# Attention and an MLP in one kernel: w_out products two units at a time, bank by bank, and a new order at the start and around the splitting of x

## The chip, the cores and the metric

The kernel runs on one core of one Trainium2 chip. The metric is device time in microseconds (us); times of a kernel are the median of several runs. Engines are named as in the profile: PE (TensorE matmul), PEld (its weight loads), DVE (VectorE), ACT (ScalarE), POOL (GpSimd), SP (SyncE, which issues all DMAs here).

## The reference

Causal attention with a decay, over 8 batches of 8 heads, 576 positions, 64 features per head, and then a two-layer MLP with a gate on 4608 tokens. Cut to what matters:

```python
scores = np.matmul(q, k.T) / 8                     # per batch and head, 576 x 576
cum = np.cumsum(np.log(np.clip(f, 1e-4, 1.0)), -1)
scores = scores + cum[:, None] - cum[None, :]      # causal: -1e9 above the diagonal
attn = exp(scores - max) / (sum + 1e-9)
x = (attn @ v) as (4608 tokens, 512)
h = x @ w_in                                       # 512 -> 2048
g = h * erf(softplus(h))
out = g @ w_out                                    # 2048 -> 512
```

## The kernel before, in words

The program has one instruction stream per engine. For PE, DVE, ACT and POOL the order of the stream is the order in which the Python code makes the instructions; each engine works through its stream in order and waits on semaphores. Only SP's stream, the DMAs, is ordered by the framework's scheduler, and it too is worked through in order: a DMA that waits for a buffer holds up all that stand behind it.

**Start.** `fd[0]` and `fd[1]` are the rows of `f` for the first two heads, broadcast to 128 partitions; `fr` is all of `f` on 64 partitions. From each, `log_clipped` (clip on DVE, log on ACT, L324 and L325) and `decay` (a running sum and a scaling on DVE, L329 and L330) make the decays. Those of the first pair of heads stay in SBUF (`c0`). Those of all heads (`cum`) are written to DRAM (`cum_d`, L482) and read back for each further pair of heads, broadcast (`c`, L344). `idle_products` (L476) are transposes of a constant that nobody reads: they keep PE running while it would have nothing to do.

**Attention** runs over 64 half pairs of heads, t = 0 to 63, as a pipeline: in iteration t stand `scores(t)` (PE, L362 and L367), `reduce(t)` (DVE, L383: adds the decays, takes the extreme), `exps(t-1)` (ACT, L395), `normalize(t-2)` (POOL, L405), `transposes(t-3)` (PE, L417) with `evacuate(t-3)` (ACT L426, DVE L422 and L424), `values(t-4)` (PE, L444) and `store(t-5)`. An even iteration transposes four banks through a ring of three, so its last bank waits for ACT's copy of its first. From t = 4 on each iteration also does a quarter of a `convert`: a piece of w_in or w_out, loaded as 64-bit floats (`wraw`, L279), is made into two float32r parts, high and low: step 0 on ACT (L289), 1 to 3 on DVE (L293, L298, L300, L303, L306) and POOL (L307).

**The MLP** (class `Moe`) works on units: 128 of the 2048 features for one block of 512 tokens. There are 14 visits of token blocks, ten with 8 units and four with 16: 144 units. For a unit j:

- `up(j)` on PE: 12 matmuls of 128x512 (L133) into one PSUM bank `ph` (ring of 4); x and the weights are split in a high and a low part, and three of the four products are made.
- `softplus(j)` and `erf(j)` on ACT (L138, L141). The two need different function tables, so several units share one change of tables (`self.ends`).
- `gate(j)`: DVE multiplies e by h (L147, after which the bank `ph` is free), makes the high part `gh` (L149), POOL the low part `gl` (L150); `gh` and `gl` have rings of 4.
- `down(j)` on PE: 12 matmuls (L169 to L171), three into each of the four banks y0 to y3, which gather a whole visit. `finish` copies the four banks out at the end of a visit (L197, L199) and stores them (L202); visits over half of the features are stored as `part_d` and added in later.

`step()` makes step j: `up(j)`, then the downs due, erf of the units due, softplus(j), the gates due, `finish`, and `split_x`. The tables `ends`, `gates` and `downs` say at which step. Before, units go in groups of three (two at either end): their erfs come at the step after the group's last up, their gates one step each from there on, and each down two steps after its gate. x of the next visit is asked for four units ahead (`want_x`), loaded in two halves through one buffer `xr` (L113), and split by ACT (`xh`, L120) and POOL (`xl`, L121). During the first 32 steps after the attention, two convert steps for the second half of the weights follow each step. `wraw` and the outputs `yo` share a ring of two buffers (`wide4`).

Of the kernel before, what the change touches and what calls it, by code (L numbers as in the profile page):

```python
# [11 lines left out]
F32 = mybir.dt.float32  # L12
# [10 lines left out]
B, H, S, D = 8, 8, 576, 64  # L23
# [44 lines left out]
class Moe:  # L68
# [8 lines left out]
    def __init__(self, tc, xt_d, out, xp, wide4):  # L77
        self.tc, self.nc = tc, tc.nc
        self.xt_d, self.out, self.xp, self.wide4 = xt_d, out, xp, wide4
        first, second, every = (list(range(*r)) for r in ((2 * NU1,), (2 * NU1, NF), (NF,)))  # L80
        self.visits = ([(c, first) for c in range(HALF)] + [(c, second) for c in range(HALF)]
                       + [(c, every) for c in range(HALF, NCH)])
        self.units = [(v, a) for v, (c, feats) in enumerate(self.visits) for a in feats]
        n = len(self.units)
        self.ends, self.gates, self.downs = {}, defaultdict(list), defaultdict(list)
        at = 0
        for size in [2] + [3] * ((n - 6) // 3) + [2, 2]:
            self.ends[at + size] = range(at, at + size)
            for k in range(size):
                self.gates[at + size + k].append(at + k)  # L90
                self.downs[at + size + k + 2].append(at + k)
            at += size
        assert at == n
        self.steps = max(self.downs) + 1
        self.w, self.x, self.e, self.gp, self.y = {}, {}, {}, {}, {}
        self.ps, self.raw, self.part, self.queue = {}, [], {}, []
        self.at = 0
# [52 lines left out]
        nc.gpsimd.tensor_tensor(out=gl, in0=e_, in1=gh.bitcast(F32), op=ALU.subtract)  # L150
        self.gp[j] = gh, gl

    def down(self, j):
        nc = self.nc
        v, a = self.units[j]
        c, feats = self.visits[v]
        gh, gl = self.gp.pop(j)
        wh, wl = (self.w[a // 2][:, i, a % 2 * DM:a % 2 * DM + DM] for i in (2, 3))
        if a == feats[0]:
            self.y[v] = [self.ps_y.tile([P, DM], F32, name=f"y{v}_{tb}", tag=f"y{tb}") for tb in range(4)]  # L160
            if a:
                self.part[v] = [self.wide4(f"part{v}_{b}").rearrange("p (a e) -> p a e", a=2) for b in range(2)]
                for b in range(2):
                    nc.sync.dma_start(out=self.part[v][b], in_=self.part_d[2 * c + b])
        y = self.y[v]
        first, last = a == feats[0], a == feats[-1]
        for tb in range(4):
            cs = slice(tb * P, tb * P + P)
            nc.tensor.matmul(out=y[tb], lhsT=gh[:, cs], rhs=wh, start=first, stop=False)  # L169
            nc.tensor.matmul(out=y[tb], lhsT=gh[:, cs], rhs=wl, start=False, stop=False)  # L170
            nc.tensor.matmul(out=y[tb], lhsT=gl[:, cs], rhs=wh, start=False, stop=last)  # L171
            if j == len(self.units) - 1:
                self.finish_last(y[tb], c * TB + tb * P)

    def finish_last(self, y, row):
# [31 lines left out]
    def step(self):  # L207
        j, n = self.at, len(self.units)
        self.at += 1
        if j < n:  # L210
            self.up(j)
            self.want_x(self.units[min(j + 4, n - 1)][0])
            self.load_x()
        for i in self.downs[j]:
            self.down(i)
        if j in self.ends:
            for i in self.ends[j]:
                self.erf(i)
            self.nc.scalar.preload_act_table_set(SOFTPLUS)
        if j < n:  # L220
            self.softplus(j)
        for i in self.gates[j]:
            self.gate(i)
        for i in self.downs[j]:
            self.finish(i)
        self.split_x()


@with_exitstack
def attention_moe(ctx, tc, q2, k2, vp, f, w_in, w_out, out):  # L230
# [84 lines left out]
    with ExitStack() as ph:  # L315
# [147 lines left out]

        fd = [wk.tile([P, S], F32, name=f"fd{j}", tag=f"pt{j}", bufs=1) for j in range(2)]
        nc.sync.dma_start(out=fd[0], in_=f[0, 0].partition_broadcast(P))
        load(0)
        nc.sync.dma_start(out=fd[1], in_=f[0, 1].partition_broadcast(P))
        fr = wk.tile([B * H, S], F32, name="fr", tag="xo")
        nc.sync.dma_start(out=fr, in_=f.rearrange("b h s -> (b h) s"))
        todo = pieces[1]  # L470

        def idle_products(t, n):
# [2 lines left out]
            for i in range(n):  # L475
                nc.tensor.transpose(out=b[:, i % 4 * P:(i % 4 + 1) * P], in_=ident, identity=ident)  # L476

        def all_decays():
            log_clipped(fr)
            cum = wk.tile([B * H, S], F32, name="cum", tag="xo")  # L480
            decay(cum, fr)
            nc.sync.dma_start(out=cum_d, in_=cum)  # L482
            load(1)
            load(2)
            load_weight(0)

        idle_products("", 16)
        log_clipped(fd[0])
        decay(pairs[0][2][:, 0], fd[0])
        log_clipped(fd[1])  # L490
        for t in range(NH + 5):
            there = [0 <= t - n < NH for n in range(6)]
            p, half = divmod(t, 2)
            if half == 0 and 0 < t < NH - 4:
                load(p + 2)
            if half == 0 and there[2]:
                load_values(p - 1)
            if NH <= t < NH + 4:
                moe.step()
            if there[2]:  # L500
                normalize(t - 2)
            if there[5]:
                store(t - 5)
            if there[0]:
                scores(t)
                if t < 3:
                    idle_products(t, 18)
            if there[1]:
                exps(t - 1, 0)
            if there[0]:  # L510
                reduce(t, 0)
                if t == 0:
                    decay(pairs[0][2][:, 1], fd[1])
            if there[3]:
                for a in range(3):
                    transposes(t - 3, a)
                evacuate(t - 3, 0)
            if there[3] and len(BANKS[(t - 3) % 2]) == 4:
                transposes(t - 3, 3)
            if there[4]:  # L520
                values(t - 4)
            if there[1]:
                exps(t - 1, 1)
            if there[0]:
                reduce(t, 1)
                if t == 0:
                    all_decays()
            if there[3]:
                for a in range(1, len(BANKS[(t - 3) % 2])):
                    evacuate(t - 3, a)  # L530
            if t >= 4 and todo:
                convert(*todo.pop(0))
            if NH - 4 <= t < NH - 2:
                moe.want_x(0)
                moe.load_x()
                moe.split_x()
            if t == NH - 1:
                early.close()
                moe.ep = moe_pools.enter_context(tc.tile_pool(name="ep", bufs=2, side="right"))
                moe.ps_h = moe_pools.enter_context(tc.tile_pool(name="ps_h", bufs=4, space=PSUM, side="right"))  # L540
# [46 lines left out]
```

## Time and profile before

| | us |
|---|---|
| median of 3 runs (lowest, highest) | 1155.87 (1155.82, 1157.66) |
| profiled execution, its own time | 1156.91 |
| its span, first to last instruction | 1155.1 |
| PE busy | 1134.1 |

PE is busy in 98% of the span and its weight loads in 80%; no other engine is in more than 54%. By stages, from the windows of the trace:

| stage | us | PE busy | ACT busy | DVE busy | granted clock |
|---|---|---|---|---|---|
| 0 to 30 (start) | 30 | 24.12 | 12.02 | 16.30 | 1.00 |
| 60 to 300 (attention) | 240 | 240.00 | 191.72 | 202.37 | 1.00 |
| 318 to 325 | 7 | 4.51 | 6.24 | 4.59 | 0.76 |
| 530 to 1130 (MLP, weights ready) | 600 | 600.00 | 240.59 | 170.46 | 1.00 |
| 1130 to 1156 (end) | 26 | 19.84 | 5.81 | 4.27 | 0.96 |

A busy PE still may run slower or faster per matmul, since matmuls overlap: what one costs is read from the distance of their starts, not from the length of one.

### The profile page before, as it was taken

The page shows a single profiled execution, that of the slowest core. Times are in us where ns is not written, and L with a number is a line of the kernel's source. Part 1 is how long each engine was busy: PE and PEld are TensorE (multiplying, and loading weights), DVE is VectorE, ACT ScalarE, POOL GpSimd, SP SyncE. Part 2 cuts the span into 40 slices and gives each one's busy share as a digit, 9 for nine tenths or more (in the row PEclk, how much of TensorE's full clock was granted, in tenths as well). Part 3 has the DMA queues.
Part 4 walks back from the last instruction along what each step waited for, and adds up shares of the span by engine and source line. Part 5 has one row for each costly group of instructions (what it writes and reads, how often), then busy time and mean ns, then how long its engine had stood idle before and what let it go on. Part 6 is the DMA issues. An engine that isn't in the chain of part 4 may idle for free.

```text
span 1155.1 us, 19541 instructions
## 1 busy us (share of the span) xinstructions
PE 1134.1 (98%) x7334; PEld 927.9 (80%) x7334; DVE 565.2 (49%) x1475; ACT 624.4 (54%) x1251; POOL 461.1 (40%) x532
## 2 busy tenths in 40 slices
PE   8999999999989999999999999999999999999998
PEld 6888888888877878778888888888888888888886
DVE  5788888888846576565233132222321322322221
ACT  3878878787786565664444344433342443243342
POOL 2556565555654445344342342332232232232121
PEclk9999999999999999999999999999999999999999
DMA  7677777777622133131031130230010010000001
GB/s 261 206 241 258 243 231 253 237 243 234 198 98 92 54 111 108 57 113 70 19 110 40 71 110 19 91 110 1 37 37 1 37 37 1 37 19 1 37 1 37
DMA packets 57726, 120.05 MB, mean 104 GB/s; under 512 B 4768, under 2 KB 20128, under 8 KB 57632
## 3 DMA queue, kind: packets, MB, share of 16 engines
q1 hardware_dynamic: 57632, 118.80, 31.4%
q8 instruction: 58, 0.95, 0.3%
q14 instruction: 36, 0.29, 0.1%
HBM read 94.52 MB, written 24.26 MB: 103 GB/s over the span
## 4 chain that ended last, share of the span: by engine, by line
PE 90%; DVE 3%; DMA 3%; ACT 2%; POOL 1%; issue 1%; SPq 0%; POOLq 0%; DVEq 0%; ACTq 0%
PE ph L133 32%; PE y L169 11%; PE y L171 11%; PE y L170 11%; PE s L362 8%; PE o L444 8%; PE t L417 7%; PE s L367 2%; DMA wraw<-in_w_in_dram 1%; POOL xl L121 1%; DVE pr L383 1%; DMA k<-in_k_dram 0%; DVE e L147 0%; ACT L289 0%; ACT L141 0%
## 5 line engine op out<-in xcount | busy, mean ns | idle before, releaser
L133 PE MATMUL ph<-xh,w 128*128 128x512 f32 x1152 | 381.7, 392 | 5.7 <-DVE e L147 5.7
L150 POOL TENSOR_TENSOR gl<-e,gh 128x512 fp32r<-128x512 f32 x144 | 186.8, 1298 | 418.9 <-DVE gh L149 414.4
L138 ACT ACTIVATE e<-ph 128x512 f32<-128x512 f32 x144 | 86.1, 598 | 385.1 <-PE ph L133 380.3
L133 PEld LDWEIGHTS ph<-xh,w 128*128 128x128 f32 x1152 | 217.2, 189 | 56.6 <-DVE e L147 5.9
L147 DVE TENSOR_TENSOR e<-e,ph 128x512 f32<-128x512 f32 x144 | 98.1, 681 | 327.0 <-ACT e L141 326.8
L169 PE MATMUL y<-w,gh 128*128 128x512 f32 x576 | 228.9, 397 | 0.0
L171 PE MATMUL y<-w,gl 128*128 128x512 f32 x576 | 228.0, 396 | 0.0
L170 PE MATMUL y<-w,gh 128*128 128x512 f32 x576 | 227.6, 395 | 0.0
L133 PE MATMUL ph<-xl,w 128*128 128x512 f32 x576 | 225.4, 391 | 0.0
L405 POOL TENSOR_SCALAR pr<-pr,st 128x576 f32<-128x576 f32 (+4 forms) x320 | 164.7, 535 | 117.8 <-DVE st L401 102.0
L395 ACT ACTIVATE pr<-pr,st 128x576 f32<-128x576 f32 (+3 forms) x320 | 176.5, 556 | 3.6 <-DVE st L383 3.5
L383 DVE CUSTOM_DVE_ANT_0 pr<-s,c 128x576 f32<-128x576 f32 (+3 forms) x320 | 136.8, 487 | 52.6 <-PE s L367 39.2
L171 PEld LDWEIGHTS y<-w,gl 128*128 128x128 f32 x576 | 108.7, 189 | 27.0
L170 PEld LDWEIGHTS y<-w,gh 128*128 128x128 f32 x576 | 108.2, 188 | 26.1
L169 PEld LDWEIGHTS y<-w,gh 128*128 128x128 f32 x576 | 108.0, 188 | 24.4
L133 PEld LDWEIGHTS ph<-xl,w 128*128 128x128 f32 x576 | 108.4, 188 | 22.7
L149 DVE CAST gh<-e 128x512 fp32r<-128x512 f32 x144 | 92.2, 640 | 66.3 <-PE y L170 52.4
L362 PE MATMUL s<-k,q 64*128 64x320 f32 (+4 forms) x768 | 110.3, 411 | 4.5 <-DVE st L383 2.5
L417 PE MATMUL t<-ident,pr 128*128 128x128 f32 x800 | 103.9, 275 | 4.2 <-ACT pt L426 2.5
L426 ACT COPY pt<-t 128x512 f32<-128x512 f32 x128 | 73.7, 577 | 61.1 <-PE t L417 61.1
L444 PE MATMUL o<-pt,v 128*64 128x128 f32 (+1 forms) x1920 | 103.8, 261 | 0.0
L444 PEld LDWEIGHTS o<-pt,v 128*64 128x64 f32 x1920 | 94.9, 138 | 9.5 <-DVE st L383 4.9
(53 smaller groups left out, 992.2 us busy)
## 6 DMA issues: line engine op xcount, KB each, us to landing
v<-in_vp_dram SPq DMA_DIRECT2D x32, 576.0 KB, 6.2
c<-cum_d SPq DMA_DIRECT2D x62, 288.0 KB, 5.0
xr<-xt_d SPq DMA_DIRECT2D x28, 512.0 KB, 3.4
q<-in_q_dram SPq DMA_DIRECT2D x32, 320.0 KB, 3.2
k<-in_k_dram SPq DMA_DIRECT2D x32, 288.0 KB, 4.2
xt_d<-xo SPq DMA_DIRECT2D x32, 288.0 KB, 5.8
wraw<-in_w_in_dram SPq DMA_DIRECT2D x16, 512.0 KB, 5.8
wraw<-in_w_out_dram SPq DMA_DIRECT2D x16, 512.0 KB, 5.6
```

What stands on the lines that cost most here:

```text
L133: nc.tensor.matmul(out=ps, lhsT=w[:, kd, fs], rhs=x[:, kd], start=kd == 0 and n == 0, stop=kd == KD - 1 and n == 2)
L147: nc.vector.tensor_mul(e_, e_, h_)
L150: nc.gpsimd.tensor_tensor(out=gl, in0=e_, in1=gh.bitcast(F32), op=ALU.subtract)
L169: nc.tensor.matmul(out=y[tb], lhsT=gh[:, cs], rhs=wh, start=first, stop=False)
L170: nc.tensor.matmul(out=y[tb], lhsT=gh[:, cs], rhs=wl, start=False, stop=False)
L171: nc.tensor.matmul(out=y[tb], lhsT=gl[:, cs], rhs=wh, start=False, stop=last)
L362: nc.tensor.matmul(out=s[j][:, at:at + k1 - k0], lhsT=q[h, PAD + START[i]:PAD + END[i]], rhs=k[h, k0:k1], start=i > 0, stop=k1 < END[i])
L383: nc.vector.tensor_tensor_reduce(out=to[:, ::-1] if j else to, in0=score, in1=decay_, scale=-0.125, scalar=BIG, op0=ALU.add, op1=ALU.min, ...
L395: nc.scalar.activation(out=seg, in_=seg, func=AF.Exp, bias=st[:, 0, j, m:m + 1], scale=-1.0, accum_out=st[:, 1, j, m:m + 1])
L405: nc.gpsimd.tensor_scalar(out=seg, in0=seg, scalar1=st[:, 2, j, m:m + 1], scalar2=1.0, op0=ALU.mult, op1=ALU.mult)
L417: nc.tensor.transpose(out=b[:, n * P:(n + 1) * P], in_=probs[t][:, at:at + P], identity=ident)
L444: nc.tensor.matmul(out=o[h, to:to + width], lhsT=v[:, ch, h], rhs=pt[:, at[j]:at[j] + width], start=n == 0, stop=n == len(parts) - 1, skip ...
```

## The change

Four things, all in the order of work; no instruction's shape or number of matmuls changes, apart from 18 more idle products at the start.

1. `down` takes two units. For each of the four banks it makes the three products of the one and then the three of the other, six in a row. Units go in twos: for an even unit a, both erfs at step a + 2, gates at a + 2 and a + 3, both downs at step a + 5 (the last two at step 146). So every other step has 24 down matmuls, and the steps between have none.
2. In `step()`, x is asked for five units ahead, and its load stands at the end of the step, behind the split.
3. Ahead of the MLP the first block of x is asked for at t = 54, and loads and splits stand at t = 54, 57 and 60, each split three iterations behind its load, instead of both at t = 60 and again at t = 61.
4. At the start `fr` is loaded second, ahead of q and k; its clip, log, sum and store to `cum_d` come ahead of the first `reduce`, not behind it; 34 idle products run ahead of the first scores, not 16.

```diff
-        at = 0
-        for size in [2] + [3] * ((n - 6) // 3) + [2, 2]:
-            self.ends[at + size] = range(at, at + size)
-            for k in range(size):
-                self.gates[at + size + k].append(at + k)
-                self.downs[at + size + k + 2].append(at + k)
-            at += size
+        for at in range(0, n, 2):
+            self.ends[at + 2] = range(at, at + 2)
+            self.gates[at + 2].append(at)
+            self.gates[at + 3].append(at + 1)
+            self.downs[min(at + 5, n + 2)] += [at, at + 1]
...
-    def down(self, j):
+    def down(self, js):
...
         for tb in range(4):
             cs = slice(tb * P, tb * P + P)
-            nc.tensor.matmul(out=y[tb], lhsT=gh[:, cs], rhs=wh, start=first, stop=False)
-            nc.tensor.matmul(out=y[tb], lhsT=gh[:, cs], rhs=wl, start=False, stop=False)
-            nc.tensor.matmul(out=y[tb], lhsT=gl[:, cs], rhs=wh, start=False, stop=last)
-            if j == len(self.units) - 1:
+            for n, (gh, gl, wh, wl) in enumerate(parts):
+                first, last = a == feats[0] and n == 0, a + 1 == feats[-1] and n == 1
+                nc.tensor.matmul(out=y[tb], lhsT=gh[:, cs], rhs=wh, start=first, stop=False)
+                nc.tensor.matmul(out=y[tb], lhsT=gh[:, cs], rhs=wl, start=False, stop=False)
+                nc.tensor.matmul(out=y[tb], lhsT=gl[:, cs], rhs=wh, start=False, stop=last)
+            if js[1] == len(self.units) - 1:
                 self.finish_last(y[tb], c * TB + tb * P)
...
             self.up(j)
-            self.want_x(self.units[min(j + 4, n - 1)][0])
-            self.load_x()
-        for i in self.downs[j]:
-            self.down(i)
+            self.want_x(self.units[min(j + 5, n - 1)][0])
+        if self.downs[j]:
+            for i in range(0, len(self.downs[j]), 2):
+                self.down(self.downs[j][i:i + 2])
...
         self.split_x()
+        self.load_x()
...
         nc.sync.dma_start(out=fd[0], in_=f[0, 0].partition_broadcast(P))
+        fr = wk.tile([B * H, S], F32, name="fr", tag="xo")
+        nc.sync.dma_start(out=fr, in_=f.rearrange("b h s -> (b h) s"))
         load(0)
         nc.sync.dma_start(out=fd[1], in_=f[0, 1].partition_broadcast(P))
...
-        idle_products("", 16)
+        idle_products("", 34)
         log_clipped(fd[0])
+        log_clipped(fr)
         decay(pairs[0][2][:, 0], fd[0])
+        cum = wk.tile([B * H, S], F32, name="cum", tag="xo")
+        decay(cum, fr)
+        nc.sync.dma_start(out=cum_d, in_=cum)
+        load(1)
+        load(2)
+        load_weight(0)
         log_clipped(fd[1])
...
                 reduce(t, 1)
-                if t == 0:
-                    all_decays()
...
-            if NH - 4 <= t < NH - 2:
+            if NH - 10 <= t < NH - 3 and t % 3 == 0:
                 moe.want_x(0)
+                moe.split_x()
                 moe.load_x()
-                moe.split_x()
```

PE's stream in the last visits, before: one unit's three products per bank (numbers behind a name tell buffers apart; `ph128` is the bank of unit 128, `gh123` the high part of unit 123, y12_0 the first bank of visit 12).

```order
L133 MATMUL ph128_9868<-xh13_9739,w0_98 128x512
L169 MATMUL y12_0_9503<-w5_5304,gh123_9832 128x512
L170 MATMUL y12_0_9503<-w5_5304,gh123_9832 128x512
L171 MATMUL y12_0_9503<-w5_5304,gl123_9833 128x512
L169 MATMUL y12_1_9504<-w5_5304,gh123_9832 128x512
L170 MATMUL y12_1_9504<-w5_5304,gh123_9832 128x512
L171 MATMUL y12_1_9504<-w5_5304,gl123_9833 128x512
```

The same place now (lines are those of the changed file); ahead of it stand the ups of units 128 and 129.

```order
L130 MATMUL ph129_9948<-xh13_9750,w0_98 128x512
L168 MATMUL y12_0_9545<-w6_5327,gh124_9877 128x512
L169 MATMUL y12_0_9545<-w6_5327,gh124_9877 128x512
L170 MATMUL y12_0_9545<-w6_5327,gl124_9878 128x512
L168 MATMUL y12_0_9545<-w6_5327,gh125_9921 128x512
L169 MATMUL y12_0_9545<-w6_5327,gh125_9921 128x512
L170 MATMUL y12_0_9545<-w6_5327,gl125_9922 128x512
L168 MATMUL y12_1_9546<-w6_5327,gh124_9877 128x512
L169 MATMUL y12_1_9546<-w6_5327,gh124_9877 128x512
L170 MATMUL y12_1_9546<-w6_5327,gl124_9878 128x512
```

A bank is left after six products instead of three, and between two runs of down products stand 24 up products instead of 12.

ACT's stream at iterations 60 and 61, before: the two splits (`xh0`, halves 0 and 1) stand one iteration apart.

```order
L120 CAST xh0_4807<-xr0_0_4809 128x4x256
L395 ACTIVATE pr60_4756,st60_4757<-pr60_4756,st60_4757 128x576
L395 ACTIVATE pr60_4756,st60_4757<-pr60_4756,st60_4757 128x192
L426 COPY pt58_4844<-t58_0_4845 128x512
L395 ACTIVATE pr60_4756,st60_4757<-pr60_4756,st60_4757 128x576
L395 ACTIVATE pr60_4756,st60_4757<-pr60_4756,st60_4757 128x192
L426 COPY pt58_4844<-t58_1_4850 128x512
L120 CAST xh0_4807<-xr0_1_4886 128x4x256
L395 ACTIVATE pr61_4837,st61_4838<-pr61_4837,st61_4838 128x448
```

Now, around the second split:

```order
L426 COPY pt57_4789<-t57_1_4795 128x512
L289 ACTIVATE wtop14_4831<-wraw14_4757 128x512
L117 CAST xh0_4362<-xr0_1_4599 128x4x256
L395 ACTIVATE pr60_4782,st60_4783<-pr60_4782,st60_4783 128x576
L395 ACTIVATE pr60_4782,st60_4783<-pr60_4782,st60_4783 128x192
```

The second split now stands at iteration 60; the first, not shown, went from iteration 60 to 57, so three iterations lie between.

SP's stream at the end of the first visit, before (`part_d` is the store of the visit's sums, `xr` a half of x, `wraw` a piece of the weights):

```order
L279 DMA wraw20_5610<-in_w_in_dram 128x2x512
L202 DMA part_d0_79<-yo0_0_5648 128x1024
L113 DMA xr2_1_5674<-xt_d_78 128x4x256
L202 DMA part_d1_80<-yo0_1_5652 128x1024
L113 DMA xr3_0_5953<-xt_d_78 128x4x256
L279 DMA wraw21_5706<-in_w_in_dram 128x2x512
L279 DMA wraw22_5784<-in_w_out_dram 128x1024
```

Now:

```order
L201 DMA part_d0_79<-yo0_0_5642 128x1024
L201 DMA part_d1_80<-yo0_1_5646 128x1024
L279 DMA wraw20_5657<-in_w_in_dram 128x2x512
L279 DMA wraw21_5744<-in_w_in_dram 128x2x512
L110 DMA xr2_1_5684<-xt_d_78 128x4x256
L279 DMA wraw22_5821<-in_w_out_dram 128x1024
```

wraw21 no longer stands behind two loads of x, and wraw20 now stands behind both stores instead of ahead of them.

More of the change, by code (lines that the diff above doesn't have):

```diff
@@ L85, in __init__ @@
         self.ends, self.gates, self.downs = {}, defaultdict(list), defaultdict(list)
-        at = 0
-        for size in [2] + [3] * ((n - 6) // 3) + [2, 2]:
-            self.ends[at + size] = range(at, at + size)
-            for k in range(size):
-                self.gates[at + size + k].append(at + k)
-                self.downs[at + size + k + 2].append(at + k)
-            at += size
-        assert at == n
+        for at in range(0, n, 2):
[3 more added lines that the diff above has]
+            self.downs[min(at + 5, n + 2)] += [at, at + 1]
         self.steps = max(self.downs) + 1
@@ L151, in gate @@
         self.gp[j] = gh, gl
-    def down(self, j):
+    def down(self, js):
         nc = self.nc
-        v, a = self.units[j]
+        v, a = self.units[js[0]]
         c, feats = self.visits[v]
-        gh, gl = self.gp.pop(j)
-        wh, wl = (self.w[a // 2][:, i, a % 2 * DM:a % 2 * DM + DM] for i in (2, 3))
         if a == feats[0]:
@@ L165, in down @@
         y = self.y[v]
-        first, last = a == feats[0], a == feats[-1]
+        parts = [(*self.gp.pop(j), *(self.w[self.units[j][1] // 2][:, i, j % 2 * DM:j % 2 * DM + DM] for i in (2, 3)))
+                 for j in js]
         for tb in range(4):
             cs = slice(tb * P, tb * P + P)
-            nc.tensor.matmul(out=y[tb], lhsT=gh[:, cs], rhs=wh, start=first, stop=False)
-            nc.tensor.matmul(out=y[tb], lhsT=gh[:, cs], rhs=wl, start=False, stop=False)
-            nc.tensor.matmul(out=y[tb], lhsT=gl[:, cs], rhs=wh, start=False, stop=last)
-            if j == len(self.units) - 1:
+            for n, (gh, gl, wh, wl) in enumerate(parts):
[4 more added lines that the diff above has]
+            if js[1] == len(self.units) - 1:
                 self.finish_last(y[tb], c * TB + tb * P)
@@ L465, in attention_moe @@
         nc.sync.dma_start(out=fd[0], in_=f[0, 0].partition_broadcast(P))
+        fr = wk.tile([B * H, S], F32, name="fr", tag="xo")
+        nc.sync.dma_start(out=fr, in_=f.rearrange("b h s -> (b h) s"))
         load(0)
         nc.sync.dma_start(out=fd[1], in_=f[0, 1].partition_broadcast(P))
-        fr = wk.tile([B * H, S], F32, name="fr", tag="xo")
-        nc.sync.dma_start(out=fr, in_=f.rearrange("b h s -> (b h) s"))
         todo = pieces[1]
@@ L476, in idle_products @@
                 nc.tensor.transpose(out=b[:, i % 4 * P:(i % 4 + 1) * P], in_=ident, identity=ident)
[L478 to L485, printed above, removed]
-        idle_products("", 16)
+        idle_products("", 34)
         log_clipped(fd[0])
+        log_clipped(fr)
         decay(pairs[0][2][:, 0], fd[0])
+        cum = wk.tile([B * H, S], F32, name="cum", tag="xo")
[4 more added lines that the diff above has]
+        load_weight(0)
         log_clipped(fd[1])
```

## The prediction, on record before the changed kernel had been run

> **What bounds the kernel now.** The page's busy times come first: PE is busy in all but 21.0 us of the 1155.1 us span, so the other engines matter only where they make PE wait.
>
> ```profile
> PE 1134.1 (98%) x7334; PEld 927.9 (80%) x7334; DVE 565.2 (49%) x1475; ACT 624.4 (54%) x1251; POOL 461.1 (40%) x532
> ```
>
> Two ways are left to get faster: fill those 21.0 us, or make the matmuls follow each other more closely. PE's own waits, read next, name four in the up products (total, times, longest); they stand at 367.7, 419.8, 465.5 and 514.1 us, all while weights are still converted. The second row, ACT's waits for weights, belongs to the last three of them.
>
> ```profile
> PE ph L133 <- DVE e L147: 5.7, 4, 2.1
> ACT L289 <- DMA wraw<-in_w_in_dram: 14.4, 3, 5.4
> ```
>
> Then the windows (length, busy time of PE, PEld, DVE, ACT, POOL, granted clock, DMA share, GB/s). In two stretches of 3.4 us the granted clock is 0.50; one follows an idle PE of 2.49 us (below), the other the 2.1 us wait above. Each costs half its length: 1.7 and 1.65 us.
>
> ```profile
> 321.20:324.60 3.40, 3.40 (x31) 3.06 (x33) 2.36 (x6) 3.04 (x11) 3.40 (x6) 0.50 0.50 162
> 356.00:530.00 174.00, 168.34 (x716) 134.89 (x715) 112.92 (x147) 110.97 (x130) 78.70 (x53) 0.99 0.25 85
> 468.00:471.30 3.30, 3.30 (x9) 2.63 (x8) 3.20 (x6) 1.82 (x2) 1.29 (x1) 0.50 0.00 0
> ```
>
> Last the timeline of PE in one undisturbed step of the MLP (start, length). Starts are what counts here.
>
> ```profile
> 703.50 0.40 PE L133 MATMUL ph<-xh,w 128*128 128x512 f32 x1
> ...
> 704.42 0.39 PE L133 MATMUL ph<-xl,w 128*128 128x512 f32 x1
> ...
> 705.10 0.39 PE L133 MATMUL ph<-xl,w 128*128 128x512 f32 x1
> ...
> 706.24 0.39 PE L169 MATMUL y<-w,gh 128*128 128x512 f32 x1
> ...
> 709.04 0.40 PE L133 MATMUL ph<-xh,w 128*128 128x512 f32 x1
> ```
>
> Inside an up run, three matmuls take 705.10 - 704.42 = 0.68 us, 0.2267 each. The 12 downs take 709.04 - 706.24 = 2.80, 0.2333 each. A unit takes 709.04 - 703.50 = 5.54, against 24 x 0.2267 = 5.44: 0.10 us over, though PE never waits. Over 144 units that is 14.4 us.
>
> **The change part by part.**
>
> *Downs bank by bank (term D).* The 0.10 us goes with the places where the output bank changes: five per unit (into y0, three between, back to ph), 0.020 each. In twos there are six per two units (one between the two ups, one into y0, three, one back) instead of ten. At 0.020 each that is 0.08 us per pair, 5.8 us for 72 pairs. The other end: the excess belongs to the down products themselves, whatever bank they write; then only the few slow matmuls at the edges of runs get rarer, 0.01 us per pair, 0.7 us. A loss is excluded by the up runs: 12 in one bank, at the closest distance of all. I lean to the first end, since the excess is absent wherever a bank is kept for long, but allow that a change costs a little more when there is time for its effect to play out: 5.0 us. The Trainium skill speaks against this term: "TensorE: Matmul & The Clock Gate", section "Back-to-back issue gap", gives a distance from the number of columns alone, N/2.4 + 2.5 = 216 ns for 512, in which a bank has no place. The trace disagrees already within one kernel (227 and 233 ns at one shape), but by that rule D would be nothing and the sum about 15 us.
>
> *Gates by twos (term C).* The chain of the second of the four waits, in the timeline:
>
> ```profile
> 412.33 0.37 SPq L113 DMA_DIRECT2D xr<-xt_d  x1
> 412.81 0.45 SPq L279 DMA_DIRECT2D wraw<-in_w_in_dram  x1
> ...
> 417.29 1.28 ACT L289 ACT_TABLE_LOAD   x1 [3.65 <-DMA wraw<-in_w_in_dram]
> ...
> 419.28 0.69 DVE L293 SCALAR_TENSOR_TENSOR wtop<-wtop,wraw 128x512 f32<-128x512 f32 x1 [4.31 <-ACT wtop L289]
> ...
> 420.72 0.47 PE L133 MATMUL ph<-xh,w 128*128 128x512 f32 x1 [0.88 <-DVE e L147]
> ```
>
> The load of x waits for its buffer, the weight load behind it in SP's queue is late, ACT waits for it, DVE's convert step waits for ACT, and the gate behind that on DVE frees the bank that up(j) needs. In the groups of three the gate of unit j stands in the step just ahead of the up that reuses its bank. In twos unit a's gate stands at step a + 2 and the bank is needed at a + 4; unit a + 1's at a + 3, needed at a + 5. Every such stretch holds a whole step more, and one of any two steps has 24 downs, 5.5 us. The narrowest place is the end of a visit, where the outputs leave through one buffer, so that DVE's third copy waits for the store of the first two:
>
> ```profile
> 405.06 1.29 DVE L199 COPY yo<-y 128x512 f32<-128x512 f32 x2 [2.80 <-DMA part_d<-yo]
> ```
>
> Counted from the end of the last downs: banks 0 and 1 end 4.2 and 2.8 us ahead of it, so they are copied (0.65 each) by -2.0, their store frees the buffer 2.80 + 0.1 later, the other two are copied by 2.3, the last convert pieces take 2 us to 4.3, wraw20 loaded 4.5 later (412.81 to 417.29) at 8.8, table 10.1, ACT 10.8, L293 11.5, gate of the second unit 12.1. Its bank is wanted after two ups, two downs and an up: 5.5 + 5.5 + 2.7 = 13.7. So 1.6 us are left, and all four waits go: 5.66 us, and the slow clock behind the third, 1.65. That is 7.3; the other end is that the margin is lost at the three visit ends and only the first wait, 1.69 us, goes. I take 7.3, the trace's row being the landing time itself. What this adds: two table changes per two units instead of per three, 1.28/3 = 0.43 us of ACT per unit, 14 us over the 32 units of the conversion, where ACT has 174 - 111 = 63 us free. `gh` and `gl` are held until the end of 24 downs; the next cast waits up to 3 us for that, but nothing needs it for 13 us. `finish` gets two ups (5.5 us) instead of one ahead of the next y0.
>
> *x's first split (term B).* The timeline near 320 us:
>
> ```profile
> 317.97 1.04 ACT L120 CAST xh<-xr 128x1024 fp32r<-128x1024 f32 x1 [2.47 <-DMA xr<-xt_d]
> ...
> 321.17 0.44 PE L417 MATMUL t<-ident,pr 128*128 128x128 f32 x1 [2.49 <-ACT pt L426]
> ```
>
> ACT stands 2.47 us for a DMA issued in the same iteration, and PE loses 2.49: nearly all of PE's gap is that wait. Loaded three iterations ahead it is gone, while the split's own 1.04 us stays on ACT, one iteration at a time. So 2.5 us and the slow clock behind it, 1.7: 4.2. Bounds: 2.5 (the clock drops anyway) to 4.2. On the clock, the same skill page ("Why this matters for your kernels") warns of idle gaps over about 3 us only; here 2.49 and 2.1 us sufficed while 1.69 did not, so the measurement decides. By the page's figure the two clock terms, 3.3 us, would have another cause and stay.
>
> *The start (term A).* The timeline again, of DVE where it makes cum,
>
> ```profile
> 15.11 1.35 DVE L329 TENSOR_TENSOR_SCAN cum<-fr 64x576 f32<-64x576 f32 x1 [0.75 <-ACT fr L325]
> 16.49 0.45 DVE L330 TENSOR_SCALAR cum<-cum 64x576 f32<-64x576 f32 x1
> ```
>
> and of all engines:
>
> ```profile
> 1.36 3.68 PE L476 MATMUL idle<-ident 128*128 128x128 f32 x16 [1.36 <-POOL ident masks.py:199]
> ...
> 19.79 3.37 SPq L344 DMA_DIRECT2D c<-cum_d  x6
> ...
> 20.98 2.13 PE L476 MATMUL idle<-ident 128*128 128x128 f32 x18
> 23.39 0.76 DVE L383 CUSTOM_DVE_ANT_0 pr<-s,c 128x576 f32<-128x576 f32 x1 [3.96 <-DMA c<-cum_d]
> ...
> 24.58 2.65 PE L362 MATMUL s<-k,q 64*128 64x448 f32 x12 [1.46 <-DVE st L383]
> ```
>
> DVE waits 3.96 us for c, then PE 1.46 for DVE. Now clip, sum and scaling of `fr` (0.45, like the scaling, + 1.35 + 0.45 = 2.25 us of DVE) stand ahead of the first reduce, which has to wait for q and k and their scores anyway: at most 2.25 us later, I reckon 0.3. cum is then done near 10 instead of 16.94 us, and c, 23.39 - 16.94 = 6.45 later, lands near 16.5, or 18 behind the fuller DMA queues of that time. The third half pair's scores end by 20.9 as now, so its reduce starts then, 2.4 us sooner; but the 18 idle products behind those scores still run until about 23.0, and the next scores start there, 1.6 sooner than 24.58, without the stop for the second head inside: 2.0 us. The 18 added idle products take 18 x 0.23 = 4.1 us at the slow clock of their row or 2.1 at the fast one, up to 8 us, where q and k land at about 7: 0 to 1 us later, made up by the faster clock of the scores behind. Bounds 0 and 3; I take 2.0.
>
> *The end (term E).* DVE's timeline of the last copies:
>
> ```profile
> 1147.77 0.42 DVE L180 COPY yo<-y 128x256 f32<-128x256 f32 x1 [8.89 <-PE y L171]
> ...
> 1151.54 0.42 DVE L180 COPY yo<-y 128x256 f32<-128x256 f32 x1 [0.56 <-DMA out_dram<-yo]
> ```
>
> Banks end three downs apart, 0.70 us, but there are two buffers, so the later copies wait for stores: the fourth starts at 1151.54, 1.67 after its bank's end (1147.77 + 3 x 0.70 = 1149.87). With 1.4 us between banks the buffers are free in time: 1.6 us; at least 1.0, if a store takes 0.6 longer.
>
> Sum: 2.0 + 4.2 + 7.3 + 5.0 + 1.6 = 20.1 us. The profiled execution took 1156.91 us, 1.8 over its span, and 1.0 over the median of 1155.87; taken off the median it gives 1136 us.
>
> **Rivals.**
> - *Banks don't matter (D is 0.7).* For it: the excess is seen on downs. Against: it fades within a few matmuls of an up run. 1136 + 4.3 = 1140.
> - *Waits move.* wraw20 now stands behind both stores in SP's queue; landing over 6.1 us instead of 4.5 uses up the margin of 1.6, and PE stops at three visit ends for 1 to 2 us, with one slow clock: 3 to 7 us, 1141. Against: SP no longer has a load of x in front.
> - *ACT becomes the bound while weights are converted* (the slower one). Per two units ACT would hold 2 x 111/32 + 0.86 = 7.8 us of 10.9. If it stood for its weights in each of 16 pairs as it now does three times (up to 5.4 us), 5.4 would make 13.2, 2.3 over, 37 us in all: 1173. It decides from 3.1 us of waiting per pair. Against: only three such waits today, all at visit ends.
> - *The start and the split gain nothing*, hidden by DVE and POOL: 1136 + 6 = 1142.
>
> **How the numbers follow.** My case 0.56, banks 0.2, moved waits 0.1, ACT 0.04, start and split 0.07, rest 0.03. My case alone runs from 1132.5 (D 6.6, A 3.0) to 1139. The range for 8 in 10 takes in banks and most of the moved waits: 1132 to 1143. Within 0.2% is 2.3 us, about what a measurement of this kernel tells from no change. All cases but ACT and part of the rest are faster by more: 0.94 faster, 0.02 same, 0.04 slower.
>
> **What would show it.** D: down products 0.227 to 0.230 us apart within a bank. C: no wait of the ups on DVE e. B: no ACT wait for xr near 318 us, granted clock 1.00 throughout. A: the reduce at 23.39 near 21, with no DMA named. E: fourth copy within 0.1 us of its bank's end. Wrong would be: downs still 0.233 apart, new waits for wraw at visit ends, or PE waiting for gl.

## The result, and the profile of the changed kernel

The changed kernel takes 1139.04 us (median of 5 runs, 1139.0 to 1141.8), the kernel before 1157.28 (median of 5, 1155.82 to 1160.88, the three of the table above among them): ratio 0.985, 95% interval 0.983 to 0.987. The profiled execution took 1139.0 us over a span of 1137.2; that of the kernel before had a span of 1155.1, so there are 17.9 us to place.

On the page PE is now busy in all but 8.2 us of the span, not 21.0 (busy time, share of the span, instructions):

```profile
PE 1129.0 (99%) x7352; PEld 928.1 (82%) x7352; DVE 563.7 (50%) x1475; ACT 694.4 (61%) x1303; POOL 459.8 (40%) x532
```

PE's waits (total, times, longest) hold none of an up product any more:

```profile
PE t L417 <- DVE pt L424: 1.8, 2, 0.9
PE s L362 <- DVE st L383: 1.5, 2, 1.2
PE idle L476 <- POOL ident masks.py:199: 1.4, 1, 1.4
```

The windows (length, busy PE, PEld, DVE, ACT, POOL, granted clock, DMA share, GB/s), first of the stretch where x is split, then of the conversion stage, have PE full and the clock at 1.00. ACT took the added table changes in its free time: 111 us became 135, more than the 14 added that were reckoned, since the window holds 62 table loads of 1.28 us instead of 46.

```profile
318.00:326.00 8.00, 8.00 (x81) 6.91 (x78) 5.25 (x23) 4.84 (x13) 5.48 (x9) 1.00 0.34 102
...
356.00:530.00 174.00, 174.00 (x756) 141.75 (x755) 109.47 (x157) 135.06 (x149) 77.20 (x55) 1.00 0.26 89
```

PE's timeline of one pair of units in the undisturbed MLP (start, length); the rows are the first up after downs, a product with the low part of x and the next such product, three on, the first down, and the first up of the next pair:

```profile
712.17 0.39 PE L130 MATMUL ph<-xh,w 128*128 128x512 f32 x1
...
713.10 0.39 PE L130 MATMUL ph<-xl,w 128*128 128x512 f32 x1
...
713.78 0.39 PE L130 MATMUL ph<-xl,w 128*128 128x512 f32 x1
...
717.63 0.39 PE L168 MATMUL y<-w,gh 128*128 128x512 f32 x1
...
723.25 0.39 PE L130 MATMUL ph<-xh,w 128*128 128x512 f32 x1
```

24 ups take 717.63 - 712.17 = 5.46 us, inside the run 0.68 for three; 24 downs take 5.62, 0.234 each. A pair takes 11.08, twice the 5.54 of before. The bank-by-bank order changed nothing here.

At the start DVE no longer names the DMA of c (in brackets: idle before, and what ended it), and the scores of t = 3 start at 22.16, not 24.58 (two of the expectations below call them the third half pair's; counted from t = 0 they are the fourth's). At the end the fourth copy starts 0.49 us after its bank's last product started, as soon as that product is over:

```profile
20.18 0.76 DVE L383 CUSTOM_DVE_ANT_0 pr<-s,c 128x576 f32<-128x576 f32 x1 [1.64 <-PE s L367]
...
22.16 1.86 PE L362 MATMUL s<-k,q 64*128 64x448 f32 x12
...
1133.14 0.40 PE L170 MATMUL y<-w,gl 128*128 128x512 f32 x1
1133.63 0.42 DVE L179 COPY yo<-y 128x256 f32<-128x256 f32 x1 [0.98 <-PE y L170]
```

Cut at the same events in both traces (the scores of t = 9, the first up, the end of the last down, the last instruction), the span divides so:

| stage (term) | before, us | changed, us | gained | predicted |
|---|---|---|---|---|
| start to the scores of t = 9 (A) | 54.47 | 51.26 | 3.2 | 2.0 |
| from there to the first up (B) | 274.94 | 270.93 | 4.0 | 4.2 |
| first up to the end of the last down (C and D) | 820.43 | 811.35 | 9.1 | 7.3 + 5.0 |
| rest (E) | 5.29 | 3.67 | 1.6 | 1.6 |
| sum | 1155.1 | 1137.2 | 17.9 | 20.1 |

### The profile page after: what moved, and what is told of

It reads as the page before. It is cut to its first block, busy times and chain, and to the rows that moved or that the text cites. A ratio compares the mean times of both kernels' runs of the same rounds, so it can differ in the third digit from the quotient of the medians.

```text
span 1137.2 us, 19614 instructions
## 1 busy us (share of the span) xinstructions
PE 1129.0 (99%) x7352; PEld 928.1 (82%) x7352; DVE 563.7 (50%) x1475; ACT 694.4 (61%) x1303; POOL 459.8 (40%) x532
## 4 chain that ended last, share of the span: by engine, by line
PE 98%; DVE 1%; DMA 0%; ACT 0%; issue 0%; DVEq 0%
PE ph L130 35%; PE y L169 12%; PE y L170 12%; PE y L168 12%; PE s L362 9%; PE o L444 9%; PE t L417 8%; PE s L367 2%; DVE pr L383 0%; DMA fd<-in_f_dram 0%; PE idle L476 0%; DVE c L329 0%; DVE pt L424 0%; DVE cum L329 0%; DVE c L330 0%
## 5 line engine op out<-in xcount | busy, mean ns | idle before, releaser
L130 PE MATMUL ph<-xh,w 128*128 128x512 f32 x1152 | 368.3, 390 | 0.0
L146 DVE CAST gh<-e 128x512 fp32r<-128x512 f32 x144 | 102.4, 711 | 62.0 <-PE y L169 47.6
L362 PE MATMUL s<-k,q 64*128 64x320 f32 (+4 forms) x768 | 107.7, 407 | 1.5 <-DVE st L383 1.5
```

Source lines behind the costliest of these rows:

```text
L130: nc.tensor.matmul(out=ps, lhsT=w[:, kd, fs], rhs=x[:, kd], start=kd == 0 and n == 0, stop=kd == KD - 1 and n == 2)
L146: nc.vector.tensor_copy(out=gh, in_=e_)
L362: nc.tensor.matmul(out=s[j][:, at:at + k1 - k0], lhsT=q[h, PAD + START[i]:PAD + END[i]], rhs=k[h, k0:k1], start=i > 0, stop=k1 < END[i])
```

## Experiments: undoing the parts

These six kernels are the changed one with one part undone. The stages are cut as above; the kernel before took 1158.7 us on the chip of the first three, 1159.51 on that of the others.

| kernel | us | A stage | B stage | C and D | rest |
|---|---|---|---|---|---|
| changed | 1139.04 | 51.26 | 270.93 | 811.35 | 3.67 |
| two units' downs one after the other | 1141.01 | 51.55 | 270.84 | 811.35 | 5.28 |
| groups of three | 1150.92 | 52.64 | 270.88 | 821.12 | 5.28 |
| x split late | 1144.37 | 51.51 | 275.58 | 811.35 | 3.68 |
| x loaded ahead of the downs | 1140.52 | 54.51 | 270.84 | 811.35 | 3.67 |
| 16 idle products | 1139.52 | 51.48 | 270.89 | 811.35 | 3.67 |
| cum after the first reduces | 1142.26 | 54.44 | 270.84 | 811.36 | 3.66 |

**Downs one unit after the other** (loops exchanged):

```diff
-        for tb in range(4):
-            for n, (gh, gl, wh, wl) in enumerate(parts):
+        for n, (gh, gl, wh, wl) in enumerate(parts):
+            for tb in range(4):
```

> The changed kernel, but the two units' downs one after the other, three per bank as before, still 24 in one step. Theory (bank changes cost nothing, the downs themselves are slower): the 24 downs take 5.64 us as in the changed kernel, a pair of units 11.08 us, the time within 0.7 us of 1139.0. Rival (the prediction's term D: each change of output bank costs 0.02 us): four more changes per pair, 0.08 us, 72 pairs, so about 5 us slower, 1144 to 1145.

A pair takes 717.84 - 706.75 = 11.09 as rounded, and the whole MLP 811.35 us in both: bank changes cost nothing. Its PE timeline, first down, first up, first down:

```profile
706.75 0.39 PE L168 MATMUL y<-w,gh 128*128 128x512 f32 x1
...
712.37 0.39 PE L130 MATMUL ph<-xh,w 128*128 128x512 f32 x1
...
717.84 0.39 PE L168 MATMUL y<-w,gh 128*128 128x512 f32 x1
```

The 1.6 us that it lost, which neither theory expected since I had left out the end, are term E: with banks three products apart the copies wait for stores again (DVE's timeline):

```profile
1134.46 0.42 DVE L179 COPY yo<-y 128x256 f32<-128x256 f32 x1 [1.66 <-DMA out_dram<-yo]
...
1135.43 0.42 DVE L179 COPY yo<-y 128x256 f32<-128x256 f32 x1 [0.55 <-DMA out_dram<-yo]
```

**Groups of three** (the old tables, single downs; the rest as changed):

```diff
-        for at in range(0, n, 2):
-            ...
+        for size in [2] + [3] * ((n - 6) // 3) + [2, 2]:
+            ...
```

> The changed kernel with part 1 undone: units in groups of three, single downs, as before; x's load order, the split and the start stay as changed. Theory (the twos keep the gates of the conversion stage ahead of the ups): PE's four waits on DVE and the slow clock come back, 7 to 9 us slower, 1146 to 1148. Rival (the waits went because the load of x now stands at the end of the step, so that the weight loads come sooner): within 1 us of 1139. A mixture shows as the wait at the first table of waits alone.

All four waits are back, as PE's waits show,

```profile
PE ph L133 <- DVE e L147: 6.3, 4, 2.6
```

and in the windows so is the slow stretch behind the third:

```profile
356.00:530.00 174.00, 167.66 (x714) 134.30 (x713) 113.75 (x150) 110.97 (x131) 76.80 (x53) 0.99 0.25 85
462.96:466.37 3.41, 3.41 (x10) 2.64 (x9) 3.31 (x6) 1.74 (x2) 1.38 (x2) 0.50 0.02 5
```

The MLP is 9.8 us longer. Together with the end's 1.6 and 1.4 of the start, where the clock was low from 15.81 to 19.22 in this execution, that is the whole difference. The twos did it.

**x loaded ahead of the downs** (part 2 undone, twos kept):

```diff
-            self.want_x(self.units[min(j + 5, n - 1)][0])
+            self.want_x(self.units[min(j + 4, n - 1)][0])
+            self.load_x()
...
-        self.load_x()
```

> The changed kernel with part 2 undone: x is asked for four units ahead and its load stands ahead of the downs. Theory (the twos alone keep the gates early enough): no wait of the ups on DVE, within 0.5 us of 1139. Rival (the load order took part of the waits away): waits of 1 to 2 us at the visit ends in the conversion stage, 2 to 6 us slower.

The MLP takes 811.35 us again: part 2 is worth nothing beside the twos. The profiled execution lost its 3.2 us at the start, which this part doesn't touch (last section); two of the four took 1139.0 and 1139.1 us, as the changed kernel did.

**x split late** (part 3 undone):

```diff
-            if NH - 10 <= t < NH - 3 and t % 3 == 0:
+            if NH - 4 <= t < NH - 2:
```

> The changed kernel with part 3 undone: the first block of x is asked for, loaded and split at t = 60 and again at t = 61. Theory (term B is a wait of ACT for that load and the clock behind it): PE's gap of 2.4 to 2.5 us near 318 us and about 3.4 us of clock 0.50 come back, 3.9 to 4.3 us slower, 1143. Rival (the start and the twos have moved the load's time, so that the wait is hidden): below 1 us. By the rule that only idle stretches over about 3 us lower the clock: 2.5 us.

The stage is 4.7 us longer, over the 3.9 to 4.3 expected, as the gap is 3.0 us this time. ACT's wait and PE's gap are back in the timeline,

```profile
315.59 1.05 ACT L117 CAST xh<-xr 128x1024 fp32r<-128x1024 f32 x1 [3.00 <-DMA xr<-xt_d]
...
318.79 0.30 PE L417 MATMUL t<-ident,pr 128*128 128x128 f32 x1 [3.02 <-ACT pt L426]
```

and in the windows the slow stretch behind them:

```profile
320.05:323.45 3.40, 3.40 (x22) 2.19 (x20) 1.72 (x5) 1.81 (x7) 3.40 (x6) 0.50 0.56 158
```

**The start's two halves.** First 16 idle products (`idle_products("", 34)` to 16), then cum back behind the second reduce, and with it the loads of the next two pairs and of the first weights, which follow its store:

> The changed kernel with 16 idle products ahead of the first scores, not 34. Theory (the start's gain is mostly the order of the sums, the idle products only bring the clock up sooner): the clock rises at about 10.5 us instead of 7.0, the third half pair's scores start 0.7 to 1.7 us later than 22.16. Rival (the idle products hold up the first scores, so fewer are better): up to 1 us sooner. In total 1139 to 1141, which the traces and not the times must tell apart.

> The changed kernel with the clip, log, sum and store of fr back behind the second reduce of the first half pair; 34 idle products and the early load of fr stay. Theory (the start's gain is the earlier cum): DVE waits for c again, the third half pair's scores start 2 to 3 us later, 1141 to 1142. Rival (it is the clock that the added idle products keep up): within 0.5 us of 1139.

With 16 idle products a slow stretch is there, but the scores of t = 3 start at 22.37 and the ups 0.18 us later, less than the 0.7 expected at least: the added products bought next to nothing. (The windows count the time ahead of a trace's first clock record, 10.57 us in the kernel before, as 1.00; its idle products there stand 0.23 us apart, against 0.12 later, which that 1.00 does not show.) With the sums moved back DVE waits for c as before, and the first up comes 3.1 us later, at 325.28 (the window is of the first kernel, the timeline rows of the second):

```profile
8.27:11.67 3.40, 3.40 (x21) 2.96 (x19) 3.37 (x8) 1.50 (x4) 0.00 (x0) 0.50 1.05 404
```

```profile
23.35 0.76 DVE L383 CUSTOM_DVE_ANT_0 pr<-s,c 128x576 f32<-128x576 f32 x1 [4.22 <-DMA c<-cum_d]
...
24.54 2.65 PE L362 MATMUL s<-k,q 64*128 64x448 f32 x12 [1.73 <-DVE st L383]
```

## Experiments: why a down is slower than an up

Term D was gone, but not the excess: 0.2 us per pair, 14.4 us in all. The gaps between starts repeat every seven downs in the same pattern, in every bank and every unit (232, 238, 237, 231, 234, 235, 233 ns), which speaks against banks, data and other engines' work as what sets them. In the built program x lies at bytes 18048 to 50816 of a partition, the weights at 67200 to 198272, every tile from a multiple of 128 on; gh, gl and e, in the pool on the right side, at 96 over a multiple of 128 (gh from 212960 on). I first thought of 64.

**32 bytes of padding**:

```diff
+        moe_pools.enter_context(tc.tile_pool(name="pad", bufs=1, side="right")).tile([P, 8], F32, name="pad")
         io = early.enter_context(tc.tile_pool(name="io", bufs=3, side="right"))
```

> The changed kernel with 32 bytes per partition reserved ahead of the pools on the right side of SBUF, so that every tile there (q, k, c; later e, gh, gl) lies 32 bytes lower, at a multiple of 64 bytes; x and w lie at such multiples already. Nothing else differs. Theory (a down takes 0.235 us instead of 0.227 because its stationary operand gh or gl lies off a 64 byte line): downs 0.227 us apart, 1728 x 0.0083 = 14.4 us faster, 1124.7. Rival (the downs' excess has another cause): within 0.7 us of 1139.

It took 1138.92 us (4 runs): no gain to speak of, and the theory as it stood fell. But the pattern had changed, to a period of two (231, 236 ns), and the MLP took 810.36 us, 0.99 less than 811.35, 0.014 per pair: the place has some effect.

**Other operands, visit by visit**, timed once:

```diff
+                if v in (6, 8):
+                    mh, ml = xh[:, tb], xl[:, tb]
+                if v in (7, 8):
+                    sh, sl = ih[:, tb, fs], il[:, tb, fs]
+                if v == 9:
+                    sh, sl = xh[:, tb, cs], xl[:, tb, cs]
+                ...
```

> The changed kernel with other operands for the downs of the visits 6 to 12 (their outputs then hold other products; number and shape of the matmuls are the same). Visit 5: as before. 6: x moves instead of w. 7: w stands instead of gh and gl. 8: both, so exactly an up's operands with the output in y. 9: x stands. 10: w of the ups moves. 11: gh stands in all three products. 12: the high part of w moves in all three. 13: as before. The excess of 0.007 to 0.008 us per down (0.234 against 0.2265) is read by visit. Theory 1 (what stands decides): gone in 7, 8 and 9, there in 6 and 10. Theory 2 (what moves decides): gone in 6 and 8, there in 7 and 9. Theory 3 (the banks y are slower than ph): there in all, 8 too. Theory 4 (gl, which POOL writes): gone in 11 alone among those with gh.

The first downs of two pairs that follow each other, in visits 5, 6 and 9:

```profile
576.58 0.39 PE L185 MATMUL y<-w,gh 128*128 128x512 f32 x1
...
587.66 0.39 PE L185 MATMUL y<-w,gh 128*128 128x512 f32 x1
...
620.90 0.39 PE L185 MATMUL y<-xh,gh 128*128 128x512 f32 x1
...
631.98 0.39 PE L185 MATMUL y<-xh,gh 128*128 128x512 f32 x1
...
752.25 0.39 PE L185 MATMUL y<-w,xh 128*128 128x512 f32 x1
...
763.13 0.39 PE L185 MATMUL y<-w,xh 128*128 128x512 f32 x1
```

11.08 with w or x moving, 10.88 with x standing; 7 and 8 gave 10.88 too, 10 to 13 gave 11.08. What stands decides, gh as much as gl, and y's banks are as fast as ph's. Theory 1 held; 2 to 4 fell.

**Other places of what stands**, timed once, and **x at the top of SBUF**, gh and gl lower. The edit of the second is:

```diff
-    xp = ctx.enter_context(tc.tile_pool(name="xp", bufs=2))
+    ctx.enter_context(tc.tile_pool(name="pad", bufs=1, side="right")).tile([P, 8], F32, name="pad")
+    xp = ctx.enter_context(tc.tile_pool(name="xp", bufs=2, side="right"))
```

> The changed kernel with other standing operands for the downs of some visits (their outputs then hold other products; number and shape of the matmuls and what moves are the same). gh and gl lie at 212960 to 229344 bytes of each partition, x at 18048 to 50816, w0 to w7 at 67200 to 198272. What stands in visit 6: the last weight tile at 190080 to 192128; 7: the same tile at 194176 to 196224; 8: at 196224 to 198272; 9: at 197760 to 198272 alone; 10: w0 in two of the four banks, gh and gl in the others; 12: the first 128 columns of gh in all banks; the other visits: gh and gl. Theory (a standing operand above 196608 bytes is loaded more slowly): a pair of units 10.88 us in 6 and 7, 11.0 to 11.08 in 8, 11.08 in 9, 10.98 in 10, 11.08 in 12. Rival (it is that gh and gl are made anew by DVE and POOL): 10.88 in 6 to 9, 11.08 in 12. Where the edge lies elsewhere between 190080 and 212960, 8 and 9 show 10.88 too, and this run doesn't tell the two apart, the next does.

> The changed kernel with the pool of x on the right side of SBUF, opened first, behind 32 bytes of padding: x lies at 192448 to 229312 bytes, and gh, gl and e, q, k and c lie 36864 bytes lower than in the padded kernel (gh and gl at 176064 to 192448), at multiples of 64 as there. No instruction differs. Theory (the place of what stands decides; what moves may lie high): downs 0.2267 us apart, a pair 10.88 us instead of 11.07, 13.4 to 14.4 us faster, 1125. Theory 2 (what moves pays for a high place too): the ups slow down instead, 1139 to 1153. Rival (freshly made gh and gl): pair 11.07 us, 1139.

In the first, visits 6 to 9 all gave 10.88, 9 with what stands above 196608, and 10 gave 10.97, half the excess: up to 198272, the highest place tried there, how high a tile lies doesn't matter. The rows are of visits 9 and 10:

```profile
748.47 0.39 PE L183 MATMUL y<-w,w 128*128 128x512 f32 x1
...
759.35 0.39 PE L183 MATMUL y<-w,w 128*128 128x512 f32 x1
...
791.99 0.39 PE L183 MATMUL y<-w,gh 128*128 128x512 f32 x1
...
802.97 0.39 PE L183 MATMUL y<-w,gh 128*128 128x512 f32 x1
```

In the second, 1140.71 us, the downs stayed slow although gh and gl lay lower, and the ups got slower (first down, first up, first down):

```profile
707.31 0.39 PE L168 MATMUL y<-w,gh 128*128 128x512 f32 x1
...
712.91 0.39 PE L130 MATMUL ph<-xh,w 128*128 128x512 f32 x1
...
718.42 0.39 PE L168 MATMUL y<-w,gh 128*128 128x512 f32 x1
```

24 ups take 5.51 us, not 5.46, a pair 11.11. The rival (gh and gl are slow because they are freshly made) fitted both runs for the downs, but not the ups: x is made as ever there, only its place is new. What x, gh and gl had in common was 64 over a multiple of 128. Hence the next run. (Slower ups are also what theory 2 had foretold: x lay high there as well as off a multiple of 128, and no run separates the two for what moves.)

**96 bytes of padding** (`[P, 24]` instead of `[P, 8]` in the first padded kernel):

> The changed kernel with 96 bytes of padding per partition on the right side of SBUF instead of the 32 of an earlier run, so that e, gh, gl (and q, k, c) start at multiples of 128 bytes. Nothing else differs. So far gh and gl stood at 96 over such a multiple (a pair of units 11.08 us) or at 64 over one (11.067 us and, with x at 64 over one too, 11.107 us with slower ups), while x and every weight tile that gave 10.88 us as what stands lie at multiples of 128. Theory (a matmul operand that starts off a multiple of 128 bytes costs PE 0.0075 to 0.0083 us per product): downs 0.2267 us apart, a pair 10.88 us, 72 x 0.2 = 14.4 us faster than the changed kernel, 1124.7. Rival (freshly made gh and gl are slow whatever their place): pair 11.07 to 11.08 us, 1139.

```profile
701.28 0.39 PE L168 MATMUL y<-w,gh 128*128 128x512 f32 x1
...
706.72 0.39 PE L130 MATMUL ph<-xh,w 128*128 128x512 f32 x1
...
712.16 0.39 PE L168 MATMUL y<-w,gh 128*128 128x512 f32 x1
```

24 downs and 24 ups take 5.44 us each, the excess is gone from every pair, and the MLP takes 797.00 us, 14.35 less. The kernel takes 1124.93 us (median of 5), 1124.7 were forecast; the ratio to the kernel before is 0.971, 95% interval 0.969 to 0.972. This version beats both. gh and gl are as freshly made here and lie almost as high as in the changed kernel, so neither of these was the cause. Not every product pays, though: q and k, which the scores take, moved with the same padding, and from the scores of t = 9 to the first up this kernel takes 270.90 us, the changed one 270.93.

**The same padding in the kernel before**:

> The kernel before with the same 96 bytes of padding and nothing else. Theory (the excess of the downs is the place of gh and gl alone, in any order of the downs): single downs 0.2267 us apart, a unit 5.440 us instead of 5.540, 144 x 0.100 = 14.4 us faster than the kernel before, 1143 in its 1157; the waits of PE in the conversion stage may grow by the time that PE arrives earlier, at most 2 us of it in 32 units. Rival (in groups of three with single downs, changes of bank still cost): only part of it, a unit above 5.45 us.

1146.75 us against 1158.88 on that chip, ratio 0.990 (0.988 to 0.991). A unit takes 5.440 us in the undisturbed stretch (first up, first down, first up), so there too it was the place and not the banks. Its PE timeline:

```profile
701.60 0.39 PE L133 MATMUL ph<-xh,w 128*128 128x512 f32 x1
...
704.32 0.39 PE L169 MATMUL y<-w,gh 128*128 128x512 f32 x1
...
707.04 0.39 PE L133 MATMUL ph<-xh,w 128*128 128x512 f32 x1
```

But only 12.1 of the 14.4 us arrive. PE's waits say why,

```profile
PE ph L133 <- DVE e L147: 7.1, 7, 2.4
```

and so does a window that ran at 1.00 before:

```profile
370.71:374.11 3.40, 3.40 (x10) 2.62 (x9) 3.26 (x6) 1.67 (x2) 2.58 (x3) 0.50 0.45 148
```

The waits on DVE grow from 5.7 to 7.1 us, and the first of them now brings a slow stretch of 3.41 us, which costs 1.7: 3.1 of the MLP's 14.4 - 11.0 = 3.4 us. With the gates by twos no up waits for DVE in the padded kernel, where a gate ends at least 1.9 us before its bank is wanted: they are what let the faster downs through.

## Why the prediction was right or wrong

1136 was forecast, 1139.04 came: inside the range, but the case that came is not the one held likeliest. Of the five terms one (D) was nothing, two (C and A) were too small, and two (B and E) came as reckoned. That the sum was off by only 2.2 us of span is in part luck: A and C brought 3.0 us more than forecast, which made up for part of the 5.0 that D did not bring.

**D, downs bank by bank: wrong.** The step that failed is "The 0.10 us goes with the places where the output bank changes". The runs showed in its place that it goes with where gh and gl start in SBUF: four more changes of bank per pair left the MLP at 811.35 us, and gh and gl at multiples of 128 bytes took 14.35 us off it. The ups served as evidence for the step, being twelve in one bank at the closest distance; but they differ from downs in their operands too, and that was not weighed. The other end named there, that the excess belongs to the down products themselves, is what the runs showed; the 0.7 us left for the edges of runs did not come either. The rival "Banks don't matter" gave 1140. What was held against it, that the excess fades within a few matmuls of an up run, goes with the place too: at multiples of 128 the first ups are as fast as the rest, and 24 of them take 5.44 us, not 5.46. Of the Trainium skill's formula weighed there ("TensorE: Matmul & The Clock Gate", section "Back-to-back issue gap", where it stands for an isolated product), the trace bears out that the bank has no place in it, while its 216 ns appeared in no run at this shape: 227 ns was the closest.

**C, gates by twos: right in mechanism, mis-sized.** 9.1 us instead of 7.3, and the groups of three brought 9.8 back. The term took the waits' own 5.66 us. Those are counted from a matmul's modelled end, 0.39 us after its start, while the next could have started 0.227 after it: four times 0.16 is 0.65 us. Three more stops of some 0.24 us, at 413.6, 459.3 and 507.9, are no rows among the waits: 0.7. The remaining 0.4 is not placed. The margin, which the prediction counted to the bank of a pair's second unit, was 2.6 us at the first visit end rather than the 1.6 worked out: the gate ended at 402.1, and its bank was wanted at about 404.7.

**B, x's first split: right**, 4.0 against 4.2, with both halves, wait and clock, in the run that undid it. That gap was 3.0 us; the term's 2.49 comes from one execution of a stop whose length varies.

**A, the start: right in mechanism, too small.** 3.2 against 2.0, over the bound of 3. The term let the 18 idle products behind the scores run until about 23.0; they started at 20.09 and were over when the next scores began at 22.16. Before, the scores ahead of them had stood for DVE, which had cum's sum in between (19.29 in its trace, 0.33 us idle); with the sum moved that stop is gone too. So the scores of t = 3 start 0.84 us sooner than the term had them; the rest lies in these scores, which took 2.65 us with their stop and take 1.86 without, 0.8 less where the term had 0.4. The run with 16 idle products shows that the 18 added ones are worth only 0.2 of it; the order of the sums, with the loads behind them, gives the rest.

**E, the end: right**, 1.6 us, and the fourth copy starts within 0.1 us of its bank's end, as forecast. **Waits moved, ACT the bound, start and split for nothing**: none of these rivals came; ACT's longest wait for weights is 3.4 us, and three such waits remain, as before. One sum on paper was off: with D at 6.6 and A at 3.0 the low end of "my case alone" is 1133.4, not 1132.5.

## What to carry to other kernels

When two loops with matmuls of one shape run at different distances, compare all that differs between them, the operands' places in SBUF among it, before the order is blamed; exchanging one operand per visit in one run separates such causes at once. Look up where the allocator puts each matmul operand, and pad a pool so that its tiles start at multiples of 128 bytes: one line, 1.2% here, more than any other part of this change. It paid for 128x512 float32r products; the scores got nothing from it, so measure which products pay. And count a stop of PE from the start that the next product could have had, not from the end drawn in the trace.

## What the runs showed of the hardware

**A place in SBUF has a price on PE.** With what stands 96 bytes over a multiple of 128, a 128x512 float32r product took 0.234 us on average in the run of downs (a pair 11.080 us), 64 over one 11.067, at a multiple 10.880. Where x, which moves in the ups, lay at 64 over a multiple, 24 ups cost 0.040 us more; it also lay high there, from 192448 on, so this is not shown to be the offset's price. Other offsets were not tried, and no run shows the mechanism behind it. The Trainium skill ("SBUF — State Buffer", section "Operand start alignment") asks only for a multiple of the element size and says that it speaks of legality, not speed; all these places are legal by it, and the runs add the price.

**The clock goes by a fixed grid.** In every trace the changes of the granted clock lie whole multiples of 3.413 us apart (92 of them from the first to the second in the run with the late split, 91 and 43 in the kernel before). Where PE stood 1.97 us or more of one such interval (by the modelled ends), the next ran at half clock, in ten cases of ten over all profiles ahead of the last downs; from 1.42 to 1.91 us either happened; at 1.39 and below never, once the clock had risen at the start. So what a stop costs depends on where it falls: in the run with the late split the gap ended at 318.79 and the slow stretch came 1.25 us later. In the run with x loaded ahead of the downs, a stop of 1.97 us at 14.37 (1.21 in the profiled run of the changed kernel) brought two slow intervals, as its window shows (why two and not one, no run tells):

```profile
15.08:21.89 6.81, 6.81 (x34) 5.94 (x32) 2.55 (x14) 3.37 (x14) 1.80 (x3) 0.50 0.69 200
```

That is its 3 us in the first stage of the table, and the likely reason why single executions of one kernel lie at 1139.0, 1140.5 or 1141.8. The Trainium skill ("TensorE: Matmul & The Clock Gate", section "What's actually happening") tells of a free-running window of 3413 ns: the trace agrees. The rule of idle gaps over about 3 us that the prediction cites from the same page of the Trainium skill, by which term B would have been 2.5, does not hold here.
